# A fused convolution and squared-ReLU MLP: when and by which queue one room of squares is written out to DRAM

## The chip, the cores and the metric

The kernel runs on one core of one Trainium2 chip. Its metric is the device time of one execution in microseconds (us), the lower the better. The core has five engines that run side by side: TensorE (PE, matrix multiply), VectorE (DVE), ScalarE (ACT), GpSimd (POOL) and SyncE (SP, which here issues transfers only). ScalarE and SyncE each issue DMA transfers into a queue of their own.

## The reference

A causal convolution with 7 taps per head (softmax over the taps), and then a two-layer MLP with a squared ReLU, over 8 x 4096 tokens of 192 features:

```python
# x: (8, 4096, 192), weight: (8 heads, 7 taps)
w = softmax(weight, axis=-1)
out[b, t, h*24 + g] = sum_k w[h, k] * x_pad[b, t + k, h*24 + g]
# then, with w_in (192, 2048), w_out (2048, 192), scalars s and b:
h = out @ w_in
r = np.maximum(h, 0.0)
g = s * (r * r) + b
return g @ w_out            # (32768, 192) float32
```

## The kernel before

**Tiling.** Features lie on the partitions, tokens along the free axis. The 192 features are split into a part A of 128 and a part B of 64. The 32768 tokens are cut into 32 pieces of 1024 (index `n`), each of two blocks of 512 (`j`), and the 2048 hidden features into eight pairs of 128 (`p`). So there are 16 steps `(n, j, p)` in each `n`.

**A step.** TensorE forms the hidden activations of one pair and one block (`first`, line 528, 36 matmuls into two PSUM banks). ScalarE takes the ReLU out of PSUM (line 556) and squares it (line 564). VectorE splits the square into a high and a low part, each precise in TensorE's fast format (lines 566 and 570). Two steps later TensorE multiplies them with the output weights of part A and adds up over the eight pairs (`second`, line 729). VectorE also computes the convolution of later blocks tap by tap (lines 181 and 183).

**Part B comes later, in batches.** For blocks from `n = 2` on, the output features of part B are not summed within the step. The square itself (`kept`) stays in memory, and every 32 steps `batch` sums four blocks at once (`second_B`, line 748: 64 matmuls of 64 x 64 tiles for a block). `evict_B` reads the sums of one block out of PSUM: ScalarE takes the two banks (lines 758 and 759), POOL adds the halves (760), SyncE moves the upper half of the partitions down (761), POOL adds again (762) and SyncE stores the result (763). The block order within a batch is `(n, 1)`, `(n + 1, 0)`, `(n + 1, 1)`, `(n, 0)` with `n` even. Sums of a block need a pair of PSUM banks, and there are two such pairs.

**Rooms.** A square lies in half of a room, a 1 MB tile of the pool `act`, with `RING = 12` rooms. A room holds the squares of two neighbouring steps, so a block takes four rooms. Of the four blocks between two batches, three stay in the twelve rooms. The first block of each even `n` does not fit: `send(n, p)` (line 577, its DMA at line 581) writes each of its rooms to DRAM, `away[n]`, once both squares of the room are there, and so gives the room back. `call_back(n)` (line 587, its DMAs at line 591) loads the four rooms again when the batch begins, through ScalarE's queue, into rooms that have come free; they are summed as the fourth block of the batch.

**Order around a batch.** `step` counts `g` from `n = 2`; `edge = g % 32` from the second such round on. At `edge` 0 the ReLU and squares of that step are put off, at `edge` 1 both steps' squares are made (in one new room), then come `call_back(n - 2)` and the four loads, then `batch`. In the step with `edge` 2, the next one, `send` is called for that new room, and in the steps 4, 6 and 8 for the other three of the block.

The instructions of VectorE, ScalarE and TensorE keep the order in which they are written (`in_order`, line 982); a DMA that ScalarE issues stands in that order too, and holds up what is written behind it while it waits. SyncE and POOL have no such rule: a planner, which works from its own estimate of times, orders their instructions, and it also decides which room a new tile gets, as rooms come free in its plan. A tile that gets a room waits on the chip until all that used the room before is done.

At the end of the kernel a last batch is written out within `step` for the final four blocks. Its squares of `(30, 0)` are called back in the same way.

Of the kernel before, what the change touches and what calls it, by code (L numbers as in the profile page):

```python
# [38 lines left out]
OLD = 2  # L39
# [9 lines left out]
def conv_attention_then_squared_relu_mlp(  # L49
# [23 lines left out]
    nc = tc.nc  # L73
# [438 lines left out]
    def add_bias():  # L512

        o, to, k = unbiased.pop(0)
        nc.scalar.activation(o, o, AF.Identity, bias=bias[0 : o.shape[0], k : k + 1])
        nc.sync.dma_start(to, o)


    def first(n, j, p, meanwhile=None):
        h = ps_h.tile([P, 2, BLK], F32, name="h")  # L520
        halves = [tok[n].half(j, i) for i in range(2)]

        def both(w, part, at, start, stop):

            for i in range(2):
                chunk = halves[i][at]
                rows = slice(i * HB, (i + 1) * HB)
                nc.tensor.matmul(  # L528
                    h[:, i, :], w_in(w, p, chunk[0], rows), chunk[part], start=start, stop=stop
                )  # L530

        for at in (0, 2, 1):
            both(0, 1, at, at == 0, False)
            both(0, 2, at, False, False)
            both(1, 1, at, False, at == 1)
            if meanwhile and at == 0:
                meanwhile()
        return h
# [20 lines left out]
    def squares(h, cast):  # L559
        return square(relu(h), cast)  # L560
# [13 lines left out]

    away, double = {}, {}

    def send(n, p):

        if p == 1:
            away[n] = far.tile([P, NPAIR // 2, 4 * BLK], F32, name="away")  # L580
        nc.sync.dma_start(
            away[n][:, p // 2], double[n, p].rearrange("p a b c -> p (a b c)")
        )
        for k in (p - 1, p):
            del kept[n, 0, k]

    def call_back(n):

        for k in range(NPAIR // 2):
            room = room_for(F32)  # L590
            nc.scalar.dma_start(room.rearrange("p a b c -> p (a b c)"), away[n][:, k])  # L591
            for i in range(2):
                kept[n, 0, 2 * k + i] = room[:, i]
        del away[n]

    def put(n, j, p, pair):
        if n >= OLD:
            kept[n, j, p] = pair[0]
            if j == 0 and n % 2 == 0 and p % 2:
                double[n, p] = two[0]  # L600
        queue.append((n, j, p, *lows(*pair)))
# [3 lines left out]
    def banks():  # L605
        return [ps_o.tile([P, BLK], F32, name=f"acc{k}") for k in (1, 2)]
# [10 lines left out]
    def out_tile(name):  # L617
        k = room[name]
        if name == "oB":
            turn[0] = 1 - turn[0]  # L620
            k += 4 * turn[0]
        return outs[:, k, :]
# [92 lines left out]
    def second(n, j, p, qh, ql):  # L715
        if n < OLD:
            return (second_split if n else second_whole)(n, j, p, qh, ql)
        if p == 0:
            acc[n, j] = banks()
        accs = acc[n, j]  # L720
        if (n, j, p) == steps[-1]:
            return last(n, j, qh, ql)

        ends = [NF - 1, NF - 1 if (n, j) != steps[-1][:2] else NF - 3]
        for f in (2 * p, 2 * p + 1):
            for w, q, lo in ((loA, qh, 0), (hiA, qh, 1), (hiA, ql, 2)):
                for i in range(2):
                    r = slice(i * HB, (i + 1) * HB)
                    nc.tensor.matmul(  # L729
                        accs[i], w(f, r), q[r, f % 2, :],  # L730
                        start=f == 0 and lo == 0, stop=f == ends[i] and lo == 2,
                    )
        if p == NPAIR - 1:
            t0 = n * SUP + j * BLK
            o, o2 = out_tile("oA"), out_tile("oA2")
            nc.scalar.activation(o, accs[0], AF.Identity, scale=sb, bias=bias[:, 0:1])
            nc.scalar.activation(o2, accs[1], AF.Identity, scale=sb)  # L737
            nc.gpsimd.tensor_tensor(o, o, o2, op=ALU.add)  # L738
            nc.sync.dma_start(outT[0:P, t0 : t0 + BLK], o)
            del acc[n, j]  # L740

    def second_B(n, j, accs):

        for p in range(NPAIR):
            q = kept.pop((n, j, p))
            for r in (slice(0, HB), slice(HB, P)):
                for i in range(2):
                    nc.tensor.matmul(  # L748
                        accs[r.start // HB][i * DB : (i + 1) * DB], WB[r, p, i, :], q[r, i, :],
                        start=p == 0, stop=p == NPAIR - 1, skip_group_check=True,  # L750
                    )
        return accs

    def evict_B(n, j, accs):

        t0 = n * SUP + j * BLK
        o, o2, oC = out_tile("oB"), out_tile("oB2"), out_tile("oC")[0:DB]
        nc.scalar.activation(o, accs[0], AF.Identity, scale=sb, bias=bias[:, 1:2])  # L758
        nc.scalar.activation(o2, accs[1], AF.Identity, scale=sb)
        nc.gpsimd.tensor_tensor(o, o, o2, op=ALU.add)  # L760
        nc.sync.dma_start(oC, o[DB:P])
        nc.gpsimd.tensor_tensor(oC, oC, o[0:DB], op=ALU.add)  # L762
        nc.sync.dma_start(outT[P:D, t0 : t0 + BLK], oC)
# [31 lines left out]
    queue = []  # L795
# [57 lines left out]
    def convolve(k):  # L853

        k += owed[0]
        owed[0] = 0
        while k > 0:
            said = next(stream, "over")
            if said in ("over", "gated"):
                return  # L860
            k -= 1
            burst[0] = k > 0
            if said == "tapped":
                owed[0] = k
                return

    def need(*what):
        while what not in ready:
            if next(stream) == "gated":
                raise ValueError(what)  # L870
# [38 lines left out]
    def batch(k):  # L909

        n = OLD + 2 * k - 2
        for block, parts in zip(((n, 1), (n + 1, 0), (n + 1, 1), (n, 0)), WINDOW):
            a = second_B(*block, banks())
            convolve(parts)
            evict_B(*block, a)

    def pace(g):
        return 0 if g % BATCH < 2 else 2 if g % BATCH in (18, 20, 22) else 1
# [5 lines left out]
    def step(n, j, p):  # L924
        now[0] = 16 * n + 8 * j + p
        if p == 0:
            if j == 0:
                need(n, "A", 0)
                need(n, "B", 0)
                tok.pop(n - 1)  # L930
            else:
                need(n, "A", 1)
        g = now[0] - 16 * OLD
        h = first(n, j, p)
        edge = g % BATCH if g >= BATCH else BATCH
        if edge == 0:
            convolve(4)
            convolve(3)
            second(*queue.pop(0))
            waiting.append((n, j, p, h))  # L940
            return
        if edge == 1:
            second(*queue.pop(0))
            *at, before = waiting.pop()
            put(*at, squares(before, nc.vector.tensor_copy))
        put(n, j, p, squares(h, nc.scalar.copy if n == OLD and p % 2 else nc.vector.tensor_copy))
        if edge == 1:
            call_back(n - 2)
        if (n, j) == (1, 1):
            if p < NPAIR - 1:  # L950
                column_sums(p + 1)
            convolve(1)
        elif n <= OLD:
            convolve(3 if n == 1 else 2)
        else:
            convolve(pace(g))
        if (n, j, p) == (2, 0, 0):
            biases()
        elif n == 2 and p % 2 == 0 and unbiased:
            add_bias()  # L960
        if (n, j, p) == steps[-1]:
            call_back(n - 1)
            a = second_B(n - 1, 1, banks())
            evict_B(n - 1, 1, a)
            for *block, evict in (n, 0, evict_B), (n - 1, 0, evict_B), (n, 1, last_B):
                h = ps_h.tile([P, 2, BLK], F32, name="h")
                evict(*block, second_B(*block, [h[:, k, :] for k in range(2)]))
            for item in queue:
                second(*item)
        while queue and len(queue) > LAG + (  # L970
            queue[0][2] == 0 and queue[0][0] <= OLD and queue[0][:2] not in ((1, 0), (OLD, 1))
        ):
            if (n, j, p) == steps[-1]:
                break
            second(*queue.pop(0))
        if edge == 1:
            batch(g // BATCH)
        sent = now[0] - 1
        if n >= OLD and sent % 32 < 8 and sent % 2:
            send(sent // 16, sent % 8)  # L980

    with in_order(nc.vector, nc.scalar, nc.tensor):
# [61 lines left out]
```

## Time and profile before

| what | before |
|---|---|
| device time, median of 3 runs | 2313.1 us (2308.86 to 2313.38) |
| the profiled execution: its own time | 2312.2 us |
| its span, first to last instruction | 2310.4 us |
| mean granted TensorE clock | 0.987 |
| write-outs (line 581), loads back (line 591) | 60 each, 1024 KB each |
| DMA traffic over the span | 243.33 MB, 105 GB/s on average |

How to read it: PE is busy with matmuls, PEld with weight loads that overlap them, and a "q" behind an engine's name is its sequencer, which issues transfers and waits. An arrow after idle time names what ended it. The tile names are the program's (`q` a square or its room, `acc` a pair of PSUM banks of sums, `outs` the output tiles, `away` the squares in DRAM, `h` the hidden activations).

### The profile page before, as it was taken

What the parts mean: (1) busy time and instruction counts of PE and PEld (TensorE: products, weight loads), DVE (VectorE), ACT (ScalarE), POOL (GpSimd) and SP (SyncE); (2) the same over time, 40 slices, a digit from 0 to 9 for tenths busy, and PEclk for the clock granted to TensorE, in tenths of its full rate; (3) what the DMA queues carried; (4) which work ended last, traced back from release to release, by engine and by line L of the source; (5) the groups of instructions that cost most, each with busy time, mean ns of one, the idle gap of its engine ahead of it and who ended that gap; (6) DMA issues with size and microseconds to landing.
All of it is one profiled execution on the core that took longest, in us unless ns stands there. A gap on an engine that the chain in (4) does not pass through costs nothing.

```text
span 2310.4 us, 44737 instructions
## 1 busy us (share of the span) xinstructions
PE 2245.4 (97%) x19334; PEld 1671.4 (72%) x19334; DVE 1605.6 (69%) x1859; ACT 1331.8 (58%) x1449; POOL 282.5 (12%) x199
## 2 busy tenths in 40 slices
PE   9999999999999999999999999999999999999999
PEld 6788668586785867858678586785867858678585
DVE  8888757677676766767667676676766757667563
ACT  8768556365563655636556365563645636456463
POOL 0010020110202002020020200202002020020201
PEclk9999999999999999999999999999999999999999
DMA  4123341423414234143331423315232152421512
GB/s 160 37 71 128 104 138 51 142 101 101 138 51 144 99 102 137 51 144 103 110 124 52 158 94 118 112 51 173 80 131 98 51 183 70 140 90 51 178 47 99
DMA packets 63286, 243.33 MB, mean 105 GB/s; under 512 B 9648, under 2 KB 9904, under 8 KB 47728
## 3 DMA queue, kind: packets, MB, share of 16 engines
q1 hardware_dynamic: 45664, 153.66, 20.7%
q10 hardware_dynamic: 17424, 86.81, 11.2%
q8 instruction: 151, 2.47, 0.4%
q14 instruction: 47, 0.39, 0.1%
HBM read 94.55 MB, written 88.08 MB: 79 GB/s over the span
## 4 chain that ended last, share of the span: by engine, by line
PE 88%; DMA 6%; ACT 3%; DVE 2%; ACTq 0%; issue 0%; SPq 0%; DVEq 0%
PE h L528 45%; PE acc L729 28%; PE acc L748 11%; DMA away<-q 6%; PE acc L675 1%; ACT q L564 1%; ACT q L556 1%; PE h L748 1%; ACT outs L758 0%; ACTq L591 0%; DVE acc L183 0%; DVE ql L570 0%; PE acc L645 0%; PE acc L651 0%; PE acc L653 0%
## 5 line engine op out<-in xcount | busy, mean ns | idle before, releaser
L556 ACT ACTIVATE q<-h 128x1024 f32<-128x1024 f32 x512 | 525.6, 1027 | 496.4 <-PE h L528 488.7
L566 DVE CAST qh<-q 128x1024 fp32r<-128x1024 f32 x482 | 343.9, 714 | 481.0 <-ACT q L564 477.8
L570 DVE TENSOR_TENSOR ql<-q,qh 128x1024 fp32r<-128x1024 f32 x498 | 623.2, 1251 | 56.1 <-ACT qh L566 4.9
L729 PE MATMUL acc<-qh,W 64*128 64x512 f32 x3816 | 587.9, 386 | 0.0
L564 ACT ACTIVATE q<-q 128x1024 f32<-128x1024 f32 x512 | 543.6, 1062 | 16.0
L748 PE MATMUL acc<-q,WB 64*64 64x512 f32 x3648 | 430.9, 621 | 58.9 <-ACT outs L758 58.9
L528 PE MATMUL h<-wB,W 64*128 64x512 f32 x1536 | 430.1, 386 | 0.0
L528 PE MATMUL h<-sB,W 64*128 64x512 f32 x1536 | 430.1, 386 | 0.0
L528 PE MATMUL h<-sA,W 64*128 64x512 f32 x3024 | 426.6, 387 | 0.0
L528 PE MATMUL h<-wA,W 64*128 64x512 f32 x3024 | 424.9, 386 | 0.0
L729 PEld LDWEIGHTS acc<-qh,W 64*128 64x128 f32 x3816 | 357.3, 184 | 75.9 <-issue 0.8
L748 PEld LDWEIGHTS acc<-q,WB 64*64 64x64 f32 x3648 | 199.0, 139 | 282.8 <-issue 170.4
L729 PE MATMUL acc<-ql,W 64*128 64x512 f32 x1908 | 371.5, 386 | 0.2 <-DVE ql L570 0.2
L528 PEld LDWEIGHTS h<-sA,W 64*128 64x128 f32 x3024 | 282.0, 184 | 70.2 <-issue 11.4
L528 PEld LDWEIGHTS h<-wA,W 64*128 64x128 f32 x3024 | 283.4, 184 | 59.5
L183 DVE SCALAR_TENSOR_TENSOR acc<-xA,tap,acc 128x512 f32<-128x512 f32 x378 | 315.9, 836 | 6.7
L528 PEld LDWEIGHTS h<-sB,W 64*128 64x128 f32 x1536 | 282.5, 184 | 30.9 <-issue 0.2
L528 PEld LDWEIGHTS h<-wB,W 64*128 64x128 f32 x1536 | 282.6, 184 | 30.1
L738 POOL TENSOR_TENSOR outs<-outs 128x512 f32<-128x512 f32 x59 | 96.0, 1627 | 1349.4 <-ACT outs L737 1349.4
L758 ACT ACTIVATE outs<-acc,bias,sb 128x512 f32<-128x512 f32 x57 | 44.5, 781 | 325.0 <-POOL outs L762 126.0
L729 PEld LDWEIGHTS acc<-ql,W 64*128 64x128 f32 x1908 | 178.8, 184 | 38.1 <-DVE ql L570 0.6
L183 DVE SCALAR_TENSOR_TENSOR acc<-xB,tap,acc 128x512 f32<-128x512 f32 x186 | 139.1, 748 | 2.5
(145 smaller groups left out, 924.8 us busy)
## 6 DMA issues: line engine op xcount, KB each, us to landing
away<-q SPq DMA_DIRECT2D x60, 1024.0 KB, 4.8
q<-away ACTq DMA_DIRECT2D x60, 1024.0 KB, 7.0
wA<-sA SPq DMA_DIRECT2D x124, 256.0 KB, 3.7
wB<-sB SPq DMA_DIRECT2D x62, 256.0 KB, 3.7
outT<-outs SPq DMA_DIRECT2D x59, 256.0 KB, 2.0
xA<-in_xA ACTq DMA_DIRECT2D x23, 515.0 KB, 3.6
outT<-outs SPq DMA_DIRECT2D x62, 128.0 KB, 2.3
xB<-in_xB ACTq DMA_DIRECT2D x30, 259.0 KB, 3.3
```

The source lines that it names most:

```text
L183: nc.vector.scalar_tensor_tensor(acc, src, w[:, k : k + 1], acc, op0=ALU.mult, op1=ALU.add)
L528: nc.tensor.matmul(h[:, i, :], w_in(w, p, chunk[0], rows), chunk[part], start=start, stop=stop)
L556: nc.scalar.activation(q, h, AF.Relu)
L564: nc.scalar.activation(q, q, AF.Square)
L566: cast(qh, q)
L570: nc.vector.tensor_tensor(ql, q, qh.bitcast(F32), op=ALU.subtract)
L675: nc.tensor.matmul(accs[to + 2 * i][0:cols], w(f, r), q[r, f % 2, :], start=start and f == 0, stop=stop and f == NF - 1,)
L729: nc.tensor.matmul(accs[i], w(f, r), q[r, f % 2, :], start=f == 0 and lo == 0, stop=f == ends[i] and lo == 2,)
L738: nc.gpsimd.tensor_tensor(o, o, o2, op=ALU.add)
L748: nc.tensor.matmul(accs[r.start // HB][i * DB : (i + 1) * DB], WB[r, p, i, :], q[r, i, :], start=p == 0, stop=p == NPAIR - 1, skip_group_c ...
L758: nc.scalar.activation(o, accs[0], AF.Identity, scale=sb, bias=bias[:, 1:2])
```

## The change

Of each even `n` from 4 on, the room of steps 0 and 1 is no longer written out in the step behind the batch by SyncE. The call moves into `batch`, behind `evict_B` of the third block, and the transfer is issued by ScalarE's queue. The rooms of the pairs 2 to 7, and all four of `n = 2`, are written out as before.

```diff
-    def send(n, p):
+    def send(n, p, queue=nc.sync):
 
         if p == 1:
             away[n] = far.tile([P, NPAIR // 2, 4 * BLK], F32, name="away")
-        nc.sync.dma_start(
+        queue.dma_start(
             away[n][:, p // 2], double[n, p].rearrange("p a b c -> p (a b c)")
         )
...
             a = second_B(*block, banks())
             convolve(parts)
             evict_B(*block, a)
+            if block == (n + 1, 1):
+                send(n + 2, 1, nc.scalar)
...
         sent = now[0] - 1
-        if n >= OLD and sent % 32 < 8 and sent % 2:
+        if n >= OLD and sent % 32 < 8 and sent % 2 and edge != 2:
             send(sent // 16, sent % 8)
```

## The prediction

> **What bounds the kernel now.** I read the page first, for the engine that sets the end.
>
> ```profile
> span 2310.4 us, 44737 instructions
> ...
> PE 2245.4 (97%) x19334; PEld 1671.4 (72%) x19334; DVE 1605.6 (69%) x1859; ACT 1331.8 (58%) x1449; POOL 282.5 (12%) x199
> ...
> PE 88%; DMA 6%; ACT 3%; DVE 2%; ACTq 0%; issue 0%; SPq 0%; DVEq 0%
> ```
>
> TensorE is busy 97% of the span and carries 88% of the chain; the other piece is a DMA with 6%, some 140 us. The groups of waits say where TensorE stands still:
>
> ```profile
> PE acc L748 <- ACT outs L758: 58.9, 14, 5.1
> ```
>
> Fourteen times, once in each batch inside the loop, 4.2 us each, before the sums of line 748. The timeline of one batch (start, duration, what; idle time in brackets), TensorE then ScalarE then SyncE:
>
> ```profile
> 418.94 13.96 PE L748 MATMUL acc<-q,WB 64*64 64x512 f32 x128
> 437.59 16.17 PE L748 MATMUL acc<-q,WB 64*64 64x512 f32 x128 [4.69 <-ACT outs L758]
> 453.69 0.96 PE L528 MATMUL h<-sA,W 64*128 64x512 f32 x6
> ```
>
> ```profile
> 420.95 1.02 ACT L556 ACTIVATE q<-h 128x1024 f32<-128x1024 f32 x1 [0.50 <-PE acc L748]
> ...
> 424.01 1.06 ACT L564 ACTIVATE q<-q 128x1024 f32<-128x1024 f32 x1
> 424.07 12.64 ACTq L591 DMA_DIRECT2D q<-away  x4
> 436.76 0.78 ACT L758 ACTIVATE outs<-acc,bias,sb 128x512 f32<-128x512 f32 x1 [11.69 <-DMA away<-q]
> ...
> 437.44 0.68 ACT L759 ACTIVATE outs<-acc,sb 128x512 f32<-128x512 f32 x1
> ```
>
> ```profile
> 425.09 0.33 SPq L581 DMA_DIRECT2D away<-q  x1
> ```
>
> TensorE sums two blocks (128 matmuls) and then has no free bank: the reading of the first block's sums, ready since about 426, starts at 436.76, because ScalarE sat 11.69 us in its queue at the four loads of line 591. The chain of waits in that stretch names the culprit, and the same in the last of the fourteen:
>
> ```profile
> 425.09 10.71 DMA away<-q
> ...
> 435.90 0.33 ACTq L591
> ...
> 436.32 0.39 ACTq L591
> ```
>
> ```profile
> 2145.45 9.64 DMA away<-q
> ...
> 2155.18 0.33 ACTq L591
> ```
>
> Two of the four loads went at once; the third left 0.1 us after the write-out of line 581 had landed, 425.09 + 10.71 = 435.80. So its room is the one which this write-out gives back: the room of the new block's steps 0 and 1. The fourth load and the reading of the sums stood behind it.
>
> **What a batch costs, and what it would cost without the stop.** The windows from the first sum of line 748 to the next matmul of line 528, for the fourteen batches (first, last and sum), then the final batch, and the 4.31 us after one stop (columns: length, busy time by engine, granted clock, DMA share, GB/s):
>
> ```profile
> 273.34:309.38 36.04, 30.99 (x258) 14.63 (x256) 14.78 (x20) 10.70 (x15) 7.52 (x6) 0.91 0.65 218
> ...
> 2139.29:2173.03 33.74, 30.12 (x259) 14.24 (x257) 19.40 (x23) 10.47 (x14) 7.84 (x6) 0.95 0.66 224
> sum 481.74, PE 422.83 PEld 196.71 DVE 260.47 ACT 143.51 POOL 98.15; mean PE 30.20 PEld 14.05 DVE 18.61 ACT 10.25 POOL 7.01
> ```
>
> ```profile
> 2273.91:2301.54 27.63, 27.63 (x258) 9.69 (x256) 2.81 (x3) 6.15 (x8) 6.25 (x5) 1.00 0.47 172
> ...
> 437.59:441.90 4.31, 4.31 (x22) 2.01 (x26) 3.18 (x4) 2.40 (x4) 1.27 (x1) 0.60 0.95 393
> ```
>
> The final batch does the same four sums over four blocks with the same four loads, but no write-out is near it, and it takes 27.63 us with TensorE never idle. The fourteen take 481.74 us, 34.41 each. The difference of 6.78 is 4.21 of idle (481.74 - 422.83 = 58.91, the whole wait above) and 2.57 of slower matmuls: after the stop the granted clock is 0.60 for 4.31 us. So the stop costs 1.6 times what it idles.
>
> **The change, part by part.** *Line 581 moves* in fourteen of the sixty write-outs (steps 0 and 1 of the even blocks from 4 on) behind the reading of the batch's third block, and from SyncE's to ScalarE's queue. Its old place ceases to matter: the room is not on offer when the loads want one, so the third and fourth load must take rooms that TensorE has read. The final batch shows how that goes:
>
> ```profile
> 2275.93 5.48 ACTq L591 DMA_DIRECT2D q<-away  x4
> 2281.45 0.78 ACT L758 ACTIVATE outs<-acc,bias,sb 128x512 f32<-128x512 f32 x1 [5.31 <-PE acc L748]
> ```
>
> Four loads, one after each room that is read (times with a plus count from the batch's first sum): +2.0 to +7.2, a room every 1.7 us (5.48 less the last issue's 0.3, by three); then the reading at +7.5. With the change the first room goes to the new block as today (the 420.95 row, +2.0), the next two to the first two loads, so the third load waits for the fourth room (+7.2) and the fourth for the fifth, of the second block (+8.9). The reading starts near +9.3 (428.2); its two halves take 1.4 us (436.76 to 437.44 and 0.68), so both banks are free at +10.7. TensorE wants them at +13.96: 3 us to spare, no stop, no slower clock. Gain: 481.74 - 14 x 27.63 = **94.9 us**. Bounds for a batch without a stop: upward 27.9, twice the 13.96 row, which counts a tail twice, 4 us in all; downward what the first 18 matmuls behind a batch take longer today than the next 18, 0.23 us, if that goes too, 3 us in all:
>
> ```profile
> 453.76 2.27 PE h L528 x18
> ...
> 457.39 2.04 PE h L528 x18
> ```
>
> *What is late next?* The called-back squares are summed as the fourth block, from +20.7. Loads land so:
>
> ```profile
> DMA to landing us min/median/max: 5.4/8.2/11.0
> ```
>
> These are the first two loads of the quoted batch, beside the write-out. The fourth load, sent at +8.9 instead of +17.4, lands by +20 even at 11.0, and its squares come last in that block, near +26. VectorE has 18.6 us of work in 34.4; its share in 27.6 still leaves 9 us.
>
> *The new issue on ScalarE.* It takes 0.33 us as in the 425.09 row, near +22, behind the third reading (sums done at +20.7). Queued behind it on ScalarE are the fourth reading (not before +27.5) and the next step's ReLU: 14 x 0.33 us lie in idle time, so I put them at nothing; uncovered they cost 4.6 us. Its squares are long done, so I see nothing it could wait for. Its landing:
>
> ```profile
> away<-q SPq DMA_DIRECT2D x60, 1024.0 KB, 4.8
> ```
>
> ```profile
> L581 SPq DMA_DIRECT2D away<-q x60: 319/332/1717, 164.5 to 2194.6; - x60
> ...
> DMA to landing us min/median/max: 3.8/5.5/11.5
> ```
>
> The issue takes up to 1.72 us there, still inside the 5 us before +27.5. The write-out lands 4.8 us behind its issue in the median; 11.5 is the longest of all write-outs and loads. I take 4.8, since the loads are over by then: +27, at worst +33.5. Its room is wanted again only if the planner picks it. SyncE's queue loses one issue, and nothing waits behind it.
>
> *The skill's word on the queue.* The Trainium skill (DMA: Bandwidth & Descriptors, Issuing engines are not separate DMA queues) says that transfers from any queue share the same 16 engines and interleave, so another queue saves issue time alone. By that rule the queue in itself is worth nothing here, and the sum would be zero if the move were only that; the 10.71 us beside two loads agree with the sharing. It speaks against the queue, not against the later moment.
>
> **The sum.** The profiled execution took 2312.2 us, 1.8 around its span; 2312.2 - 94.9 = 2217.3. The median of the runs shown is 0.9 higher: **2218 us**.
>
> **The rivals.**
>
> *The output chain comes late.* The fourth reading stands behind POOL and SyncE:
>
> ```profile
> 445.50 1.42 POOL L762 TENSOR_TENSOR outs<-outs 64x512 f32<-64x512 f32 x1 [6.04 <-DMA outs<-outs]
> ...
> 453.10 1.26 POOL L762 TENSOR_TENSOR outs<-outs 64x512 f32<-64x512 f32 x1 [4.50 <-DMA outs<-outs]
> ```
>
> ```profile
> 454.40 0.78 ACT L758 ACTIVATE outs<-acc,bias,sb 128x512 f32<-128x512 f32 x1 [5.08 <-POOL outs L762]
> 455.64 0.69 ACT L759 ACTIVATE outs<-acc,sb 128x512 f32<-128x512 f32 x1 [0.47 <-POOL outs L760]
> 456.23 1.02 ACT L556 ACTIVATE q<-h 128x1024 f32<-128x1024 f32 x1
> ```
>
> ```profile
> 439.49 0.47 SPq L761 DMA_DIRECT2D outs<-outs  x1
> ...
> 450.81 0.46 SPq L761 DMA_DIRECT2D outs<-outs  x1
> ```
>
> Before each last sum of POOL (line 762) lies a transfer of SyncE (line 761): 6.0 us from issue to sum beside the loads (439.49 to 445.50), 2.3 without (450.81 to 453.10). The fourth reading waits for the second of these and already trails TensorE by 0.7 us. With the change the chain begins 8.5 us earlier, TensorE is ready 7.1 earlier, but the write-out crosses the second transfer: if it then takes 6.0 as well, the reading trails by 0.7 + 3.7 - 1.4 = 3.0, and the ReLU behind it by some 2.5. How much of that TensorE feels:
>
> ```profile
> 459.17 2.25 DVE L570 TENSOR_TENSOR ql<-q,qh 128x1024 fp32r<-128x1024 f32 x1
> ```
>
> ```profile
> 462.67 0.62 PE L729 MATMUL acc<-qh,W 64*128 64x512 f32 x4
> ```
>
> The squares of that step are ready at 461.42, TensorE takes them at 462.67: 1.2 us of slack. So 1.3 us a batch at worst: up to 2236. Against it: the median write-out is over in 4.8. Chance 0.13.
>
> *A later room.* The planner chooses rooms by its own clock. At worst the fourth load gets the second block's last room (+14), the reading starts at +14.4, TensorE 0.8 later (436.76 to 437.59): a stop of 1.3 us, 18 us in all, 2236. If the clock falls as now, 2.57 more each: 2272. Against it: the final batch takes rooms in the order read. The Trainium skill (TensorE: Matmul & The Clock Gate, Why this matters for your kernels) warns of idle gaps over about 3 us; by it 2236 holds and not 2272. The stop of 4.69 us with 0.60 behind it agrees; no stop in this trace is as short as 1.3. Chance 0.14.
>
> *It does nothing.* Were the third load held by traffic, not by the room, it would be as late again: 2313. Against it: it leaves 0.1 us after that landing in both batches quoted. This is also what the rule on queues alone would give. Chance 0.06.
>
> *Slower.* The planner hands the write-out's room to the next step's ReLU, and ScalarE waits for a landing that now comes late. ReLU is due near +30 and has the 1.2 us of slack; to eat the 6.8 us as well, the landing must come after +38, 16 us behind the issue, when 11.5 is the longest. With 20 us it would be 14 x 4 slower, 2368. Chance 0.05.
>
> **How the numbers follow.** Forecast 0.62, the rivals as said. Low: 2218 less 3 and some runs' spread, 2209; high: the output chain and the later room without clock loss, 2245; beyond lie the half of the later room's cases, doing nothing and slower. 0.2% is about what a measurement of this kernel tells from no change. Faster 0.62 + 0.13 + 0.14 = 0.89, same 0.06, slower 0.05.
>
> **What would show it.** Right: line 748 waits for line 758 nowhere; the write-out leaves the chain; the batches take 27.6 us at a clock of 1.00; the four loads leave by +9. Wrong: idle time before line 748 with another releaser, a gap before line 528 or 729 behind the batch (output chain), or loads spread to +14 (later room).

## The result, and the profile after

| | before | after |
|---|---|---|
| device time, median of 5 runs each | 2313.38 us (2308.86 to 2314.39) | 2219.51 us (2218.83 to 2221.03) |
| ratio, 95% interval | | 0.9598 (0.9584 to 0.9612) |
| span of the profiled execution | 2310.4 us | 2217.7 us |
| mean granted clock | 0.987 | 1.000 |

The forecast was 2218. The page after, its busy shares and its chain:

```profile
span 2217.7 us, 44710 instructions
...
PE 2211.8 (100%) x19334; PEld 1609.7 (73%) x19334; DVE 1615.8 (73%) x1859; ACT 1332.3 (60%) x1449; POOL 291.2 (13%) x199
...
PE 98%; DVE 2%; DMA 0%; ACT 0%; issue 0%; SPq 0%; DVEq 0%; ACTq 0%
```

The DMA has left the chain, which is now TensorE's but for the 2% of VectorE that stood in it before. The timelines of the second batch, TensorE and then ScalarE, beside those of before:

```profile
411.20 27.70 PE L748 MATMUL acc<-q,WB 64*64 64x512 f32 x256
438.82 0.98 PE L528 MATMUL h<-sA,W 64*128 64x512 f32 x6
```

```profile
416.33 4.08 ACTq L591 DMA_DIRECT2D q<-away  x4
420.45 0.78 ACT L758 ACTIVATE outs<-acc,bias,sb 128x512 f32<-128x512 f32 x1 [3.13 <-PE acc L748]
...
434.02 0.33 ACTq L581 DMA_DIRECT2D away<-q  x1
440.63 0.78 ACT L758 ACTIVATE outs<-acc,bias,sb 128x512 f32<-128x512 f32 x1 [5.92 <-POOL outs L762]
```

All four blocks are one run of 256 matmuls where there were two of 128 with a stop between them. The four loads take 4.08 us of ScalarE's queue instead of 12.64. The third and the fourth alone, in the view of line 591 cut to two short windows:

```profile
L591 ACTq DMA_DIRECT2D q<-away x1: 326/326/326, 418.4 to 418.4; - x1
```

```profile
L591 ACTq DMA_DIRECT2D q<-away x1: 326/326/326, 420.1 to 420.1; - x1
...
DMA to landing us min/median/max: 13.2/13.2/13.2
```

That is +7.2 and +8.9 behind the batch's first sum at 411.20, and the reading begins at +9.25. The windows of the fourteen batches, cut as before, with their sum:

```profile
411.20:438.82 27.62, 27.62 (x258) 9.69 (x256) 19.70 (x23) 10.19 (x13) 5.93 (x4) 1.00 0.79 279
...
sum 386.77, PE 386.77 PEld 135.71 DVE 264.62 ACT 143.21 POOL 86.88; mean PE 27.63 PEld 9.69 DVE 18.90 ACT 10.23 POOL 6.21
```

Every batch takes 27.6 us with TensorE never idle and a clock of 1.00. The batches gave 481.74 - 386.77 = 94.97 us. The span fell by 92.7 only, so the rest of the kernel grew from 1828.7 us (2310.4 - 481.74) to 1830.9 (2217.7 - 386.77): 2.3 us were given back outside the batches.

### The profile page after: what moved, and what is told of

The parts are those of the page before. It is cut to its first block, busy times and chain, and to the rows that moved or that the text cites. A ratio compares the mean times of both kernels' runs of the same rounds, so it can differ in the third digit from the quotient of the medians.

```text
span 2217.7 us, 44710 instructions
## 1 busy us (share of the span) xinstructions
PE 2211.8 (100%) x19334; PEld 1609.7 (73%) x19334; DVE 1615.8 (73%) x1859; ACT 1332.3 (60%) x1449; POOL 291.2 (13%) x199
## 4 chain that ended last, share of the span: by engine, by line
PE 98%; DVE 2%; DMA 0%; ACT 0%; issue 0%; SPq 0%; DVEq 0%; ACTq 0%
PE h L528 46%; PE acc L729 29%; PE acc L748 18%; PE acc L675 2%; PE h L748 1%; DVE acc L183 0%; DVE ql L570 0%; PE acc L645 0%; PE acc L651 0%; PE acc L653 0%; PE acc L652 0%; PE acc L644 0%; PE acc L647 0%; DMA xA<-in_xA 0%; DVE q L308 0%; DVE q L322 0%
## 5 line engine op out<-in xcount | busy, mean ns | idle before, releaser
L566 DVE CAST qh<-q 128x1024 fp32r<-128x1024 f32 x482 | 339.4, 704 | 483.4 <-ACT q L564 458.8
L748 PE MATMUL acc<-q,WB 64*64 64x512 f32 x3648 | 394.9, 590 | 0.0
L183 DVE SCALAR_TENSOR_TENSOR acc<-xA,tap,acc 128x512 f32<-128x512 f32 x378 | 323.9, 857 | 6.7
L748 PEld LDWEIGHTS acc<-q,WB 64*64 64x64 f32 x3648 | 138.1, 133 | 248.9 <-issue 248.9
```

Source lines behind the costliest of these rows:

```text
L183: nc.vector.scalar_tensor_tensor(acc, src, w[:, k : k + 1], acc, op0=ALU.mult, op1=ALU.add)
L566: cast(qh, q)
L748: nc.tensor.matmul(accs[r.start // HB][i * DB : (i + 1) * DB], WB[r, p, i, :], q[r, i, :], start=p == 0, stop=p == NPAIR - 1, skip_group_c ...
```

## Was it the room, the queue, or the traffic?

The theory: the third load takes the room that the write-out gives back, so what counts is when that transfer has landed, or that the planner does not offer the room at all. The rivals: ScalarE's queue is worth something in itself; the later place in the text is enough; or the 1 MB written beside the loads slows them whatever the room.

**The later place, but SyncE issues.**

```diff
             if block == (n + 1, 1):
-                send(n + 2, 1, nc.scalar)
+                send(n + 2, 1, nc.sync)
```

> The call stands behind the reading of the third block as in the changed kernel, but SyncE issues it. Theory (room): what counts is whether the room is on offer when the third load asks; SyncE's order is the planner's, which puts the transfer back to the moment at which the squares are done, so third load, stop and time are those of before: 2313 us, 14 stops of about 4.2 us. Rival (place in the text): the later place is enough by itself, 2220 us.

One run: 2315.4 us beside 2312.2 of the kernel before. The chain of waits in its second batch:

```profile
425.06 10.85 DMA away<-q
...
436.00 0.33 ACTq L591
```

The planner orders SyncE's transfers, and it set this one where it had been (425.06, and 425.09 before). The later place in the text alone does nothing; on ScalarE, whose order is the text's, the same line has an effect.

**SyncE issues, tied behind its last store of the third block.**

```diff
             if block == (n + 1, 1):
-                send(n + 2, 1, nc.scalar)
+                with behind(nc.sync):
+                    send(n + 2, 1, nc.sync)
```

> SyncE issues the write-out, but tied behind SyncE's last store of the third block's output. Theory (room): late enough, so the third and fourth load take rooms that TensorE has read; batches of 27.6 us, 2217 to 2222 us. Rival (queue): the gain came from ScalarE's queue, so 2313 us.

One run: 2217.2 us, span 2215.4. The gain does not need ScalarE's queue; a late moment is enough. The Trainium skill (DMA: Bandwidth & Descriptors, Issuing engines are not separate DMA queues) has transfers of all queues share the same engines, so that another queue saves issue time alone; this run agrees in so far as the whole gain is there without ScalarE's queue, 2217.2 us beside 2219.5. ScalarE's queue served only to hold the transfer back.

**ScalarE issues ahead of the loads.**

```diff
-            if block == (n + 1, 1):
-                send(n + 2, 1, nc.scalar)
...
         if edge == 1:
+            send(n, 1, nc.scalar)
             call_back(n - 2)
```

> ScalarE issues the write-out ahead of the four loads, at about +5.1 us. By the order of the waits the third load again takes its room. Theory (room, and the time of its landing): alone in front of the loads it lands within about 5 us, near +10, the first reading starts near +11 and TensorE, which wants the banks at +13.96, does not stop: 2218 to 2224 us. Rival (any early write-out brings the stop back, since loads and write share the engines): landing near +16 as before, 2313 us.

One run: 2231.2 us. ScalarE in its second batch (first sum at 412.20), and the view of the transfers of `away` there, the write-out and the first two loads:

```profile
418.36 0.33 ACTq L581 DMA_DIRECT2D away<-q  x1
418.73 5.36 ACTq L591 DMA_DIRECT2D q<-away  x4
424.14 0.78 ACT L758 ACTIVATE outs<-acc,bias,sb 128x512 f32<-128x512 f32 x1 [5.81 <-DVE acc L181]
```

```profile
L581 ACTq DMA_DIRECT2D away<-q x1: 332/332/332, 418.4 to 418.4; - x1
...
DMA to landing us min/median/max: 4.8/8.2/10.1
```

Ahead of the loads the write-out, the shortest of the three, lands in 4.8 us instead of 10.71, the four loads leave within 5.4, and the first reading starts at +11.9, two microseconds before TensorE wants the banks. So an early write-out into the same room is harmless in the batch if it lands soon: fourteen batches take 387.94 us here, 1.2 more than in the changed kernel. The time lies above my range of 2218 to 2224, since 12.8 us (2229.4 - 387.94 = 1841.5, against 1828.7) are lost outside the batches; that is the output chain, below.

**A small early write-out.** In the kernel before, the early transfer carries 128 of 2048 columns, into a DRAM tile of its own; the squares of steps 2 and 3 stand in for those of 0 and 1, which the part-B sums lack.

```diff
+    far2 = ctx.enter_context(tc.tile_pool(name="far2", bufs=2, space=bass.MemoryType.DRAM))
...
-        nc.sync.dma_start(
-            away[n][:, p // 2], double[n, p].rearrange("p a b c -> p (a b c)")
-        )
+        room = double[n, p].rearrange("p a b c -> p (a b c)")
+        if p == 1 and n > OLD:
+            spare = far2.tile([P, BLK // 4], F32, name="spare")
+            nc.sync.dma_start(spare, room[:, 0 : BLK // 4])
+        else:
+            nc.sync.dma_start(away[n][:, p // 2], room)
+        if p == 3 and n > OLD:
+            nc.sync.dma_start(away[n][:, 0], room)
```

> The kernel before, but from the second set on the early write-out of steps 0 and 1 is 128 of 2048 columns (64 KB instead of 1 MB), so the room is free soon; in place of the squares of steps 0 and 1 those of steps 2 and 3 are written twice, which leaves the former out of the part-B sums. Queue and moment are those of before. Theory (the stop lasts until the write-out has landed): landing near +8.5, the loads leave by +9, the first reading starts before +10, no stop, 2215 to 2225 us. Rival (an early issue on SyncE's queue is harmful as such): stops as before, 2313 us.

One run: 2217.0 us. Queue and place are those of before. The transfer leaves 2.0 us sooner (+4.15 instead of +6.15, since its columns belong to the first of the room's two squares) and lands by +5.7 in this batch. ScalarE's four loads take 4.48 us and the batches have no stop.

```profile
415.46 4.48 ACTq L597 DMA_DIRECT2D q<-away  x4
419.99 0.78 ACT L764 ACTIVATE outs<-acc,bias,sb 128x512 f32<-128x512 f32 x1 [3.48 <-DVE acc L184]
```

The room has another reader, VectorE's subtraction of the second square (line 571 here), and that one ends last now. The second load is the one that waits: it leaves at 418.64, behind the end of this row (417.34 + 1.23 = 418.57), and in all fourteen batches 0.07 to 0.08 us behind it.

```profile
417.34 1.23 DVE L571 TENSOR_TENSOR ql<-q,qh 128x1024 fp32r<-128x1024 f32 x1
```

**The traffic without the room.** The changed kernel, with a second, idle copy of the same room written by SyncE at the old moment.

```diff
+    far2 = ctx.enter_context(tc.tile_pool(name="far2", bufs=2, space=bass.MemoryType.DRAM))
...
         if edge == 1:
+            spare = far2.tile([P, 4 * BLK], F32, name="spare")
+            nc.sync.dma_start(spare, double[n, 1].rearrange("p a b c -> p (a b c)"))
             call_back(n - 2)
```

> The changed kernel with a second, idle copy of the same 1 MB written by SyncE at the old moment, so the traffic beside the loads is that of before while the room comes free late. Theory (room): the loads leave by +9, no stop; the loads land 2 to 3 us later, the output chain perhaps too: 2217 to 2232 us. Rival (traffic): what delayed the batch was the 1 MB written beside the loads, so near 2313 us.

One run: 2249.2 us, span 2247.5, outside both expectations. The batches stay whole (TensorE idles 0.4 us in all fourteen together), so the stop is the room's and not the traffic's; but the copy has a price of its own, paid outside them (columns of the windows as before):

```profile
sum 388.08, PE 387.68 PEld 135.11 DVE 258.24 ACT 143.34 POOL 83.68; mean PE 27.69 PEld 9.65 DVE 18.45 ACT 10.24 POOL 5.98
```

388.08 is 1.3 us more than without the copy; 2247.5 - 388.08 = 1859.4 is 30.7 more than the 1828.7 of before.

**How early may ScalarE issue it?** Behind the first reading instead of the third:

```diff
-            if block == (n + 1, 1):
+            if block == (n, 1):
                 send(n + 2, 1, nc.scalar)
```

> ScalarE issues the write-out behind the reading of the first block's sums, near +11 instead of +23. Theory (room): the four loads stand ahead of it and keep the rooms that TensorE has read; batches of 27.6 us and no stop. Now the write-out crosses the first transfer of the output chain instead of the second, so the fourth reading may trail as far as in the changed kernel: 2216 to 2228 us. Rival (behind the third reading is what matters): the stop comes back, 2313 us.

One run: 2218.9 us, as the changed kernel. That it stands behind the loads in ScalarE's order is what matters, not which block's sums it follows.

## What is paid behind the batches

The fourth reading of a batch waits for the output chain (POOL, a transfer of SyncE, POOL). After the change, SyncE's two transfers of line 761 with the first block's store (line 763) between them, and POOL's sums of line 762 that wait for them:

```profile
423.56 0.46 SPq L761 DMA_DIRECT2D outs<-outs  x1
...
432.27 0.49 SPq L763 DMA_DIRECT2D outT<-outs  x1
435.18 0.46 SPq L761 DMA_DIRECT2D outs<-outs  x1
```

```profile
430.98 1.26 POOL L762 TENSOR_TENSOR outs<-outs 64x512 f32<-64x512 f32 x1 [7.45 <-DMA outs<-outs]
...
439.31 1.29 POOL L762 TENSOR_TENSOR outs<-outs 64x512 f32<-64x512 f32 x1 [5.32 <-DMA outs<-outs]
```

From issue to sum the first takes 7.4 us beside the loads, the second 4.1 beside the write-out (6.0 and 2.3 before). The fourth reading starts at 440.63, 1.8 us behind TensorE's next work at 438.82, where before it was 0.7.

The store is a link of this chain that the prediction left out. The upper halves of all blocks go through one output tile (`oC`), so the second transfer waits until the first block's store has landed: here that takes 2.9 us (432.27 to 435.1), and in all fourteen batches the transfer leaves 0.05 to 0.07 us behind that landing.

Whether the late reading is the loss can be told by moving the write-out away from the second transfer. The tied version does so:

```profile
433.82 0.46 SPq L761 DMA_DIRECT2D outs<-outs  x1
...
443.92 0.58 SPq L581 DMA_DIRECT2D away<-q  x1
```

```profile
438.03 0.98 PE L528 MATMUL h<-sA,W 64*128 64x512 f32 x6
```

```profile
438.19 0.78 ACT L758 ACTIVATE outs<-acc,bias,sb 128x512 f32<-128x512 f32 x1 [4.46 <-PE acc L748]
```

There the write-out leaves 10 us behind the second transfer, and the fourth reading waits for TensorE, as it should, 0.2 us behind. Both kernels were timed on one chip:

> The changed kernel once more, timed on the chip on which the next one is timed: 2217 to 2222 us, ratio to before 0.958 to 0.961.

> The write-out on SyncE's queue, tied behind SyncE's last store of the third block's output (near +35 instead of +23), timed. Theory: the 2 us that the changed kernel lost behind the batches came from the write-out crossing the output chain's second transfer; here it crosses nothing that ScalarE waits for, so 1.5 to 2.5 us less than the changed kernel on the same chip, 2215 to 2219 us. Rival: the one look at it fell well by chance, no difference.

The changed kernel: 2219.32 us (2218.77 to 2219.43), ratio 0.9597 (0.9584 to 0.9610). The tied one: 2217.62 us (2217.02 to 2217.76), ratio 0.9590 (0.9577 to 0.9603). The intervals against before overlap, but the runs of the two do not: 1.7 us. This is the better version, by 0.08%.

The changed kernel shows the same from batch to batch. From the third batch on, where the fourth reading is 1.1 to 1.2 us late, the stretch to the next batch takes 109.06 or 109.07 us, as it does in the tied kernel; where it is 1.8 to 1.9 us late, from the second batch on, it takes 109.11 to 109.33. Not all of the 2.3 us are the chain's: 0.8 lie ahead of the second batch, which starts at 411.20 here and at 410.40 in the tied kernel. In the other profiled execution of the changed kernel it starts at 410.58, so most of this part does not recur.

Last, the idle copy again with the tied write-out, to see which part of its price came through ScalarE's queue:

```diff
             if block == (n + 1, 1):
-                send(n + 2, 1, nc.scalar)
+                with behind(nc.sync):
+                    send(n + 2, 1, nc.sync)
```

> The idle copy at the old moment again, with the real write-out tied on SyncE's queue as in held_sync_timed. If the 30 us that the idle copy cost come from the later landing of the output chain's first transfer beside loads and copy, most of them stay: 2235 to 2250 us. If they come from ScalarE waiting at the write-out in its queue for the fourth load's landing, they go: 2216 to 2222 us.

One run: 2229.2 us, span 2227.5, between the two expectations; neither held. How late the fourth reading is in four kernels, in the second batch of each: TensorE's next matmul of the hidden layer, and then the reading.

```profile
439.35 0.98 PE L529 MATMUL h<-sA,W 64*128 64x512 f32 x6
```

```profile
442.08 0.78 ACT L759 ACTIVATE outs<-acc,bias,sb 128x512 f32<-128x512 f32 x1 [6.79 <-POOL outs L763]
```

```profile
440.09 0.98 PE L529 MATMUL h<-sA,W 64*128 64x512 f32 x6
```

```profile
444.13 0.78 ACT L759 ACTIVATE outs<-acc,bias,sb 128x512 f32<-128x512 f32 x1 [7.55 <-POOL outs L763]
```

```profile
443.45 0.97 PE L528 MATMUL h<-sA,W 64*128 64x512 f32 x6
```

```profile
446.69 0.78 ACT L758 ACTIVATE outs<-acc,bias,sb 128x512 f32<-128x512 f32 x1 [7.17 <-POOL outs L762]
```

```profile
439.83 0.98 PE L528 MATMUL h<-sA,W 64*128 64x512 f32 x6
```

```profile
442.73 0.78 ACT L758 ACTIVATE outs<-acc,bias,sb 128x512 f32<-128x512 f32 x1 [5.16 <-POOL outs L762]
```

The first pair is the copy with the tied write-out, the second the copy with ScalarE's, the third the exchanged readings of the next section, the fourth the write-out ahead of the loads. With the sums of their windows (386.79 us for the tied kernel without copy, 388.23 with it, 410.00 for the exchanged readings at a span of 2266.0) this makes a price list, where the loss is the span less the fourteen batches, less 1828.7, by fourteen:

| kernel | fourth reading behind TensorE, second batch | mean of the fourteen | lost per batch, outside its window |
|---|---|---|---|
| tied | 438.19 - 438.03 = 0.2 us | 0.2 us | 0.0 us |
| changed | 440.63 - 438.82 = 1.8 | 1.6 | 0.16 |
| copy, tied | 442.08 - 439.35 = 2.7 | 2.5 | 0.76 |
| write-out ahead of the loads | 442.73 - 439.83 = 2.9 | 2.5 | 0.91 |
| exchanged readings | 446.69 - 443.45 = 3.2 | 3.5 | 1.95 |
| copy, ScalarE's queue | 444.13 - 440.09 = 4.0 | 3.7 | 2.2 |

By the means, up to some 1.8 us cost next to nothing, and what lies beyond that costs about as much as it is late. The copy's 30.7 us are thus 10.6 that it costs wherever the write-out stands, and some 20 that come only with the write-out in ScalarE's queue. The 10.6 come mostly through the first block's store. The chain of waits in the copy with the tied write-out, second batch:

```profile
432.86 5.47 DMA outT<-outs
...
438.41 2.22 DMA outs<-outs
```

With the copy this store lands in 4.6 us in the mean of the batches, in the tied kernel without copy in 2.4; the first transfer lands 0.7 us later (7.9 instead of 7.2), and the second in 2.2 us in both. With the write-out in ScalarE's queue beside the copy, the second transfer takes longer too, 3.5 us in the mean. In the exchanged readings it is the store again: the write-out leaves 0.1 us behind it, and the store lands in 4.9 us in the mean.

In the copy's run on ScalarE's queue the write-out also left late; ScalarE was free at 436.58 (435.89 + 0.69):

```profile
435.89 0.69 ACT L760 ACTIVATE outs<-acc,sb 128x512 f32<-128x512 f32 x1 [0.90 <-POOL outs L761]
438.12 0.33 ACTq L582 DMA_DIRECT2D away<-q  x1
```

What held it for 1.5 us was the landing of the fourth load, which left at 421.3 and landed 16.8 us later, at 438.1:

```profile
L592 ACTq DMA_DIRECT2D q<-away x1: 326/326/326, 421.3 to 421.3; - x1
...
DMA to landing us min/median/max: 16.8/16.8/16.8
```

In thirteen of the fourteen batches the write-out leaves 0.02 us behind that landing. In the changed kernel the fourth load has landed 0.7 to 4.1 us before the write-out is issued. Why the write-out waits for that load stays open.

## What a short stop costs

The forecast charged each stop with 2.57 us of slower matmuls and put them to the clock. Two kernels make a stop on purpose. The first ties the first reading behind the second block's last sum:

```diff
+    tiny = late.tile([P, 1], F32, name="tiny")
...
             a = second_B(*block, banks())
+            if block == (n, 1):
+                held_back = a
+                convolve(parts)
+                continue
+            if block == (n + 1, 0):
+                nc.scalar.copy(tiny, a[1][:, 0:1])
+                evict_B(n, 1, held_back)
             convolve(parts)
             evict_B(*block, a)
```

> The changed kernel with the first reading tied behind the second block's last sum, which makes a stop of about 1.2 us in each of the fourteen batches (the rival of the later room, made on purpose; a copy of one column more on ScalarE). Two theories of what a short stop costs: with a fall of the granted clock as behind the stops of before, a batch takes 27.63 + 1.2 + 2.6 = 31.4 us; without one, 27.63 + 1.2 = 28.8 us and a granted clock of 1.00. The output chain starts 5 us later as well, which may cost 1 to 3 us a step group behind the batch: in all 2235 to 2280 us.

The second exchanges the two readings:

```diff
             a = second_B(*block, banks())
             convolve(parts)
+            if block == (n, 1):
+                held_back = a
+                continue
             evict_B(*block, a)
+            if block == (n + 1, 0):
+                evict_B(n, 1, held_back)
```

> The changed kernel with the readings of the first and second block exchanged in ScalarE's order, so that the third block waits some 2.5 us for its banks in each batch. With a fall of the clock: 27.63 + 2.5 + 2.6 = 32.7 us a batch; without: 30.1 us at 1.00. Read by the batches, since the output chain moves too; in all 2250 to 2300 us.

One run each: 2244.4 and 2267.8 us. The first one's TensorE and its window:

```profile
414.26 13.96 PE L749 MATMUL acc<-q,WB 64*64 64x512 f32 x128
429.21 14.53 PE L749 MATMUL acc<-q,WB 64*64 64x512 f32 x128 [0.99 <-ACT outs L759]
```

```profile
414.26:443.67 29.41, 28.42 (x258) 13.43 (x257) 19.44 (x23) 10.07 (x14) 5.36 (x4) 1.00 0.71 262
```

The stop is 0.99 us, the batch 1.78 longer than 27.63, and the clock stays at 1.00. So 0.8 us of slower matmuls comes with this stop, without the clock. Behind it the matmuls start two at a time, the second two 0.48 us behind the first, where in the changed kernel they start four at a time. So likely it is the second bank, read 0.7 us behind the first; that is argued from the order, not shown. The exchanged readings stop TensorE for 0.86 us only, not 2.5, with 29.29 us a batch, also at 1.00:

```profile
428.99 14.53 PE L748 MATMUL acc<-q,WB 64*64 64x512 f32 x128 [0.86 <-ACT outs L758]
```

```profile
428.16 0.78 ACT L758 ACTIVATE outs<-acc,bias,sb 128x512 f32<-128x512 f32 x1 [2.13 <-PE acc L748]
```

ScalarE's first reading there is the second block's, and TensorE goes on as it ends (428.16 + 0.78 = 428.94): the third block begins in the second block's banks. My size for that stop was wrong; the reading of it is the same.

The shortest stop of before whose row I have is 3.6 us, in the last of the fourteen batches, and its window has a mean clock of 0.95:

```profile
PE acc L748 <- ACT outs L758: 3.6, 1, 3.6
```

The Trainium skill (TensorE: Matmul & The Clock Gate, Why this matters for your kernels) warns of gaps above about 3 us between bursts of matmuls: 1.0 without a fall and 3.6 with one agree, and nothing here lies between.

## Why the prediction was right, point by point

- **The bound and its releaser: right.** The wait before line 748 is gone and the write-out has left the chain. That the third load waited for the room was an inference from 0.1 us in two batches. It is 0.10 to 0.15 us in all fourteen, and two runs together show it: the traffic without the room (the idle copy) makes no stop, and neither does the room without the long transfer (the small early write-out).
- **The new room order: right to the tenth.** Third load +7.2, fourth +8.9, first reading +9.3 were forecast from the final batch; measured +7.2, +8.9 and +9.25.
- **The batch: right.** 27.63 us forecast, 386.77 / 14 = 27.63 measured; 94.9 us forecast, 94.97 measured. The lower bound had no ground: the first 18 matmuls behind a batch (a step of line 528 has 18, not 36) still take 2.29 us, at full clock and without a stop, so their 0.23 us were never the stop's.

```profile
438.89 2.29 PE h L528 x18
```

- **The split of a stop: wrong in part.** The sum of 2.57 us stands, but the clock has only 4.31 x 0.40 = 1.7 of it; 0.8 comes with the stop at full clock. Nothing in the forecast hung on it but the price of the later room: made on purpose, a stop of 1.0 us gives 2244, between the 2236 and 2272 given for 1.3 us.
- **The loads' landing: missed.** The fourth load took 13.2 us, beyond the 11.0 taken as its worst, and landed at +22.1 instead of by +20 in this batch. It had until near +26.
- **The new issue: right at nothing.** It took 0.33 us at +22.8. "I see nothing it could wait for" was too strong: in the run with the idle copy it waited for the fourth load's landing.
- **The output chain: a rival that came true in small.** It was a case with up to 18 us; it bit in the forecast case too, as part of the 2.3 us. It put the second transfer at 6.0 us and the reading 3.0 late, where 4.1 and 1.8 were measured, and it did not see that this transfer waits for the first block's store. Its slack, 1.2 us beyond the 0.7 by which the reading trailed already, fits the price list. This is the term that the sum lacked: 2217.3 was forecast for the profiled execution, 2219.5 came. That the stated 2218 lies closer is luck, since its 0.9 us for the median of other runs had nothing to do with the change; here the profiled execution is the median.
- **Slower, and nothing done:** neither. The second is what the same line does on SyncE.

## What to carry to other kernels

When an engine sits in its queue at a load into a recycled room, ask which transfer gives that room back, and compare with a place in the same trace where the transfer is missing: the final batch here gave the new time to a tenth. A stop of TensorE costs more than it idles, so price it from whole stages. Behind a planner, moving a line need not move anything: put the transfer on an engine whose order is the text's, or tie it, and then look at what it crosses at its new moment, and at which transfers wait for those that it crosses.

## What was not expected of the hardware

In the batches quoted, a transfer of 128 KB between partitions (line 761) needs 2.3 us from issue to the sum that waits for it when it is alone, 4.1 beside one write-out of 1 MB and 7.4 beside the four loads. A 1 MB write-out lands in 4.8 us ahead of two loads in the same queue and in 10.71 beside them from the other queue.
